# Seven block products in the second expert chunk, and the gate's first steps among the attention's last matmuls

## The chip, the core and the metric

One core of a Trainium2 chip runs one program. The time is what the device takes for it, in microseconds (us). TensorE (PE) multiplies matrices, VectorE (DVE), ScalarE (ACT) and GpSimd (POOL) work element by element, and SyncE (SP) issues most of the transfers from memory.

## The reference

Three layers in a row, all in float32: attention with sinks and a sliding window, a mixture of 8 experts whose weights P are normalised over rows and columns eight times, and a second two-layer network.

```python
scores = where(is_sink | in_window, q @ k.T / sqrt(D), -1e9)
a = exp(scores - max); a /= sum(a); x = a @ v            # 2 x 8 heads, 768 tokens, D = 64

P = exp(x @ w_gate - max)                                # 1536 tokens, 512 wide, 8 experts
for _ in range(8):
    P /= P.sum(1) + 1e-9; P /= P.sum(0) + 1e-9; P *= N / E
for e in range(8):                                       # w1: 512 x 1024, w2: 1024 x 512
    out += P[:, e] * (maximum(x @ w1[e], 0) @ w2[e])

g = maximum(out @ w_in, 0) ** 2                          # 512 x 2048
return g @ w_out
```

## The kernel before, in words

**Chunks and blocks.** The hidden width is cut into chunks of 512: 16 expert chunks (two for each expert) and 4 of the last network. The 1536 tokens are three blocks of 512 (t = 0, 1, 2). A chunk's first layer makes h from x and w1, the second layer adds h @ w2 to acc. Each float32 operand is kept as a high and a low part (`xh`, `xl`, weights `h`, `l`), and a product is three matmuls, high by high and the two mixed ones; `pair_split` (L467) makes such a pair with an ACT copy for the high part and a POOL subtraction for the low part.

**Plain and fast first layers.** `plain(c, t, f)` is one group of 12 matmuls of 512 columns: a quarter f of the chunk's width for block t. `fast(c, half, 0)` (L780) makes blocks 0 and 1 together for two quarters by seven block products (p1 to p7, 6 matmuls each) instead of eight, in the manner of Strassen and Winograd. It needs sums of weights (S1 to S4: `unit_sums` on POOL, then `units(c, half, 3, k)` splits them into pairs) and sums of x (T1 to T4: `sums(0)`, subtractions on DVE followed by a `pair_split`). Its additions are steps e1 to e7: e1 copies p1's bank to the scratch tile x0 on ACT, and p2 goes on adding in that bank; the others are DVE additions, and p3 and p4 go on adding in the banks that e5 and e7 read. Scratch tiles have one buffer for each tag ("x0", "x1", "x2", "u"); a tag's next tile waits until the last reader of the one before is done. `sums(1)` and `fast(c, half, 1)` do the same inside block 2.

**What is fast.** Chunk 0 runs among the attention's steps (phase_a, `filler`), in groups of 384 tokens. Chunk 1 is plain in all three blocks, in the order 1, 0, second layer of 1, then 2, second layer of 0 and 2. From chunk 2 on (`is_fast`) the first layer goes by products. The sums T of x are made during chunk 1, since all later expert chunks use the same x.

**Order of work.** It is written out by hand: every engine runs its instructions in the order in which the program issues them. In phase_b `run` goes through a list `seq` of PE groups; `plan[k]`, filled with `put(k, step)`, holds what is issued after group k. `gate()` (L933) is a generator of 13 pauses: three steps with 8 matmuls each for the logits, one for the largest logit, two more, and then the eight normalisations, one for each pause. `GATE_AT` lists after which groups its next step is issued. Its matmuls take the weights `wgz` (tag x0), made from the load `wgr` (tag x2) by an ACT copy and a DVE subtraction (L1304, L1305).

**The start of phase_b.** The loads' memory is that of the attention, so they start when its last matmuls have read theirs. `next_loads` issues the loads in the order of `load_list`, each into one of three buffers; load number k waits until number k - 3 has been used. Then `wgr` is issued. The `fill` loop issues what is left of chunk 0's matmuls; after each finished group it calls `evac` and one of four `units` steps. After it come the copies for `wgz`, then `run` with one plain group and the last three groups of chunk 0 (`rest`), then the list of chunk 1:

```python
        for _ in fill:                       # L1295
            if self.done:
                self.evac()
                if todo:
                    todo.pop(0)()
        ...
        gate = self.gate()                   # L1308
```

Of the kernel before, what the change touches and what calls it, by code (L numbers as in the profile page):

```python
# [10 lines left out]
F32 = mybir.dt.float32  # L11
# [3 lines left out]
AF = mybir.ActivationFunctionType  # L15
ALU = mybir.AluOpType
# [21 lines left out]
NC = NC1 + NC2  # L38
CONV = 3
CONV_AT = (0, 1, 2, 3, 8, 9, 10, 11, 12, 13, 14, 15)  # L40
GATE_AT = (0, 1, 2, 3, 5, 7, 9, 11, 13, 16, 19, 22, 25, 30)
W2_AT = (2, 5, 8, 11)
NB = 512
BIG = 1e30
# [4 lines left out]
class Kernel:  # L49
# [373 lines left out]
    def load_list(self, c0):  # L423

        loads, k = [(c0, which, half) for which in range(2) for half in range(2)], 0
        for c in range(c0, NC):
            wide = [(j, 2, 0) for j in range(k, min(k + CONV, 8 * NC2)) if c >= 2]
            k += len(wide)
            n = c + 1
            loads += wide[0:1]  # L430
            if n < NC:
                if self.is_fast(n):
                    loads += [(n, 3, 0), (n, 3, 1)]
                loads += wide[1:2] + [(n, 0, 0)] + wide[2:3] + [(n, 0, 1), (n, 1, 0), (n, 1, 1)]
            else:
                assert len(wide) < 2
        return loads
# [217 lines left out]
        o = 2 * NB * q + w * t  # L655
        return tuple(x[:, k : k + 2, o : o + w] for x in (self.xh, self.xl))

    def sums(self, q):

        nc = self.nc  # L660
        T = [
            self.tp.tile([128, 3, 2, NB >> q], F32R, tag=f"T{q}{t}", name=f"T{q}{t}")
            for t in "hl"
        ]
        self.T[q] = T

        def tt(o, a, b, op):
            if isinstance(o, str):
                o = self.scratch2(o)[:, 0 : NB >> q]
            nc.vector.tensor_tensor(out=o, in0=a, in1=b, op=op)  # L670
            return o

        B = {n: self.operand(n, q) for n in ("B11", "B12", "B21", "B22")}
        f32 = lambda n, hl, kc: B[n][hl].bitcast(F32)[:, kc]

        def put(name, kc, x):
            hi, lo = self.operand(name, q)
            self.pair_split(hi[:, kc], lo[:, kc], x)

        for kc in range(2):  # L680
            x = tt("x0", f32("B22", 0, kc), f32("B12", 0, kc), ALU.subtract)
            y = tt("u", f32("B22", 1, kc), f32("B12", 1, kc), ALU.subtract)
            yield
            t3 = tt("x2", x, y, ALU.add)
            put("T3", kc, t3)
            yield
        for kc in range(2):
            x = tt("x0", f32("B12", 0, kc), f32("B11", 0, kc), ALU.subtract)
            y = tt("u", f32("B12", 1, kc), f32("B11", 1, kc), ALU.subtract)
            yield  # L690
            t1 = tt(x, x, y, ALU.add)
            put("T1", kc, t1)
            yield
            t2 = tt("u", f32("B22", 0, kc), t1, ALU.subtract)
            tt(t2, t2, f32("B22", 1, kc), ALU.add)
            put("T2", kc, t2)
            yield
            t4 = tt("x2", f32("B21", 0, kc), t2, ALU.subtract)
            tt(t4, t4, f32("B21", 1, kc), ALU.add)
            put("T4", kc, t4)  # L700
            yield
# [564 lines left out]
    def phase_b(self, c0, first, fill):  # L1266
# [25 lines left out]
        nc.gpsimd.memset(self.ones, 1.0)  # L1292
        nc.sync.dma_start(out=wgr, in_=self.wg)
        todo = [partial(self.units, c0, half, 0, k) for half in range(2) for k in range(2)]
        for _ in fill:  # L1295
            if self.done:
                self.evac()
                if todo:
                    todo.pop(0)()
        self.evac()  # L1300
        for step in todo:
            step()
        hz = self.wgz[:, :, 0:E]
        nc.scalar.activation(out=hz, in_=wgr, func=AF.Copy)  # L1304
        nc.vector.tensor_tensor(  # L1305
            out=self.wgz[:, :, E : 2 * E], in0=wgr, in1=hz.bitcast(F32), op=ALU.subtract
        )
        gate = self.gate()  # L1308
        groups = itertools.count()

        def run(seq, plan):

            for k, g in enumerate(seq):
                g()
                for step in plan.get(k, ()):
                    step()
                if next(groups) in GATE_AT:
                    next(gate, None)

        conv = itertools.chain.from_iterable(self.wide(k) for k in range(8 * NC2))  # L1320
# [3 lines left out]
        for c in range(c0, NC):  # L1324
# [6 lines left out]

            off = 0
            if not low:
                run([self.plain(c, 1, 0), *rest], {})
                low = first.close() or True
                self.w2p = self.pool(left, "w2" + n)
                self.tp = self.pool(left, "T" + n)
                self.cp, self.T = self.pool(left, "c" + n), {}
                seq = [self.plain(c, t, f) for t in (1, 0) for f in range(KD)][1:]
            elif self.is_fast(c):  # L1340
                seq = self.fast(c, 0, 0) + self.fast(c, 1, 0)
            else:
                seq = [self.plain(c, t, f) for t in (1, 0) for f in range(KD)]
            for k in range(4):
                put(W2_AT[k] if self.is_fast(c) else k, self.part_w2, c, k)
            if c == NC1:
                x = [self.x2(2, kc) for kc in range(KD)]
                seq = sum(([s, *x[k : k + 1]] for k, s in enumerate(seq)), [])
            m = len(seq)
            if self.is_fast(c):  # L1350
                (a, b, *e), (f, g, *i) = (self.fast(c, half, 1) for half in range(2))
                if c < FAST2:
                    seq += self.second(c, 1) + [a, b, f, g]
                else:
                    seq += [a] + self.second(c, 1) + [b, f, g]
                early = 4 if c < FAST2 else 2
                for k, step in (
                    (early, e[0]), (early, e[5]), (early, e[4]), (4, e[6]), (5, e[1]), (5, e[2]),
                    (6, i[0]), (6, i[5]), (6, i[4]), (6, i[6]), (6, e[3]),
                    (7, i[1]), (7, i[2]), (7, i[3]),  # L1360
                ):
                    put(m + k, step)
            else:
                seq = seq + self.second(c, 1) + [self.plain(c, 2, f) for f in range(KD)]
            if c == NC1 - 1:
                x = [self.x2(t, kc) for t in (1, 0) for kc in range(KD)]
                seq += sum(
                    ([s, x[k]] for k, s in enumerate(self.second(c, 0) + self.second(c, 2))), []
                )
                wide = lambda k: m + k if k < 8 else m + 2 * k - 8  # L1370
            else:
                seq += self.second(c, 0) + self.second(c, 2)
                wide = lambda k: m + k
            if c in (FAST - 1, FAST2 - 1):
                t = self.sums(0)
                for k in range(13):
                    put(k if c < FAST else min(2 * k, k + 5), next, t, None)
                t = self.sums(1)
                for k in range(13):
                    put(m + 8 + k // 2, next, t, None)  # L1380
            if c + 1 < NC:
                if self.is_fast(c + 1):
                    for half in range(2):
# [105 lines left out]
```

## Time and profile before

| | us |
|---|---|
| runs before: median of 3 | 1380.14 (1380.13 to 1380.63) |
| profiled execution | 1378.92 |
| its span | 1377.1 |
| PE busy | 1363.8 (99%), 7105 matmuls |
| DVE busy | 953.6 (69%) |
| ACT busy | 453.8 (33%) |
| POOL busy | 501.8 (36%) |

The span is what the profiler saw between the first and the last instruction of that execution. Busy time is the union of an engine's instructions; waiting instructions are not counted. Matmuls overlap in PE's pipeline, so a matmul of 512 columns has a duration of about 0.39 us while the next one starts 0.23 us after it. In a row of a time line, "x4" is that many instructions in a row, and the bracket at the end tells how long the engine stood idle before them and which instruction ended that.

### The profile page before, as it was taken

The page shows a single profiled execution, that of the slowest core. Times are in us where ns is not written, and L with a number is a line of the kernel's source. Part 1 is how long each engine was busy: PE and PEld are TensorE (multiplying, and loading weights), DVE is VectorE, ACT ScalarE, POOL GpSimd, SP SyncE. Part 2 cuts the span into 40 slices and gives each one's busy share as a digit, 9 for nine tenths or more (in the row PEclk, how much of TensorE's full clock was granted, in tenths as well). Part 3 has the DMA queues.
Part 4 walks back from the last instruction along what each step waited for, and adds up shares of the span by engine and source line. Part 5 has one row for each costly group of instructions (what it writes and reads, how often), then busy time and mean ns, then how long its engine had stood idle before and what let it go on. Part 6 is the DMA issues. An engine that isn't in the chain of part 4 may idle for free.

```text
span 1377.1 us, 18909 instructions
## 1 busy us (share of the span) xinstructions
PE 1363.8 (99%) x7105; PEld 1142.8 (83%) x7105; DVE 953.6 (69%) x1884; ACT 453.8 (33%) x1007; POOL 501.8 (36%) x442
## 2 busy tenths in 40 slices
PE   8999999999999999999999999999999999999998
PEld 5777888888888888888888888888888888888887
DVE  8777368887777777777777768765454568866564
ACT  6776322322232222222232222222232243433331
POOL 4322136534343434424343434423343035543310
PEclk9999999999999999999999999999999999999999
DMA  5232210132313232232313232230102010111101
GB/s 205 82 87 73 78 31 31 62 103 65 124 54 112 77 95 85 92 107 68 117 54 121 71 96 81 92 107 32 61 32 77 16 62 16 62 52 57 46 24 72
DMA packets 61146, 102.53 MB, mean 74 GB/s; under 512 B 3956, under 2 KB 43252, under 8 KB 60788
## 3 DMA queue, kind: packets, MB, share of 16 engines
q1 hardware_dynamic: 61040, 101.22, 23.3%
q8 instruction: 58, 0.95, 0.3%
q14 instruction: 44, 0.36, 0.1%
q10 hardware_dynamic: 4, 0.00, 0.0%
HBM read 89.67 MB, written 11.53 MB: 73 GB/s over the span
## 4 chain that ended last, share of the span: by engine, by line
PE 79%; DVE 1%; ACT 0%; issue 0%; DVEq 0%; ACTq 0%
PE mm L900 42%; PE mm L749 36%; PE mm L917 0%; ACT tx L720 0%; DVE acc L640 0%; DVE tx L721 0%; ACT hh L732 0%; DVE tx L809 0%; DVE hl L733 0%; DVE acc L636 0%; DVE mm L721 0%; DVE raw L565 0%; ACT tx L823 0%; DVE raw L552 0%; DVE tu L809 0%
## 5 line engine op out<-in xcount | busy, mean ns | idle before, releaser
L900 PE MATMUL mm<-w2h,hh 128*128 128x512 f32 (+1 forms) x916 | 356.9, 390 | 0.0
L900 PE MATMUL mm<-w2l,hh 128*128 128x512 f32 (+1 forms) x916 | 355.9, 389 | 0.0
L900 PE MATMUL mm<-w2h,hl 128*128 128x512 f32 (+1 forms) x916 | 355.7, 388 | 0.0
L469 POOL TENSOR_TENSOR w2l<-raw,w2h 128x512 fp32r<-128x512 f32 x76 | 118.4, 1557 | 366.0 <-ACT w2h L468 364.1
L640 DVE SCALAR_TENSOR_TENSOR acc<-mm,P,acc 128x512 f32<-128x512 f32 x168 | 125.7, 748 | 135.5 <-PE mm L900 134.2
L900 PEld LDWEIGHTS mm<-w2h,hl 128*128 128x128 f32 x916 | 172.0, 188 | 35.8
L900 PEld LDWEIGHTS mm<-w2h,hh 128*128 128x128 f32 x916 | 172.1, 188 | 34.5
L900 PEld LDWEIGHTS mm<-w2l,hh 128*128 128x128 f32 x916 | 172.1, 188 | 34.4
L512 POOL TENSOR_TENSOR raw<-raw 128x256 f32<-128x256 f32 x136 | 125.5, 926 | 8.8 <-DVE m L544 0.8
L469 POOL TENSOR_TENSOR s0l<-raw,s0h 128x512 fp32r<-128x512 f32 (+1 forms) x36 | 45.5, 1265 | 199.5 <-ACT s0h L468 199.5
L717 ACT ACTIVATE hh<-tx 128x512 fp32r<-128x512 f32 (+1 forms) x112 | 58.9, 525 | 130.0 <-DVE tx L809 129.5
L809 DVE TENSOR_TENSOR tx<-mm,tu 128x512 f32<-128x512 f32 (+1 forms) x136 | 75.6, 556 | 20.9 <-PE mm L749 16.7
L809 DVE TENSOR_TENSOR tx<-mm,tx 128x512 f32<-128x512 f32 (+1 forms) x68 | 37.9, 557 | 56.8 <-PE mm L749 55.5
L727 DVE SCALAR_TENSOR_TENSOR hl<-tx,hh 128x512 fp32r<-128x512 f32 (+1 forms) x112 | 70.1, 626 | 9.8 <-ACT hh L717 9.8
L823 ACT ACTIVATE tx<-mm 128x512 f32<-128x512 f32 x34 | 20.4, 599 | 156.6 <-PE mm L749 154.7
L633 DVE TENSOR_TENSOR acc<-mm,acc 128x512 f32<-128x512 f32 (+1 forms) x49 | 33.2, 677 | 50.8 <-PE mm L900 50.5
L717 ACT ACTIVATE hh<-mm 128x512 fp32r<-128x512 f32 (+1 forms) x68 | 34.1, 502 | 99.7 <-PE mm L749 99.7
L823 ACT ACTIVATE txs<-mm 128x256 f32<-128x256 f32 x34 | 13.0, 382 | 151.3 <-PE mm L749 151.3
L469 POOL TENSOR_TENSOR a0l<-raw,a0h 128x512 fp32r<-128x512 f32 (+1 forms) x38 | 42.6, 1137 | 51.8 <-ACT a0h L468 47.5
L749 PE MATMUL mm<-xl,a1h 128*128 128x512 f32 (+1 forms) x172 | 60.3, 350 | 0.2 <-ACT tx L823 0.2
L749 PE MATMUL mm<-xl,a0h 128*128 128x512 f32 (+1 forms) x172 | 59.8, 348 | 0.0
L749 PE MATMUL mm<-xh,a0h 128*128 128x512 f32 (+1 forms) x172 | 59.8, 347 | 0.0
(262 smaller groups left out, 3149.8 us busy)
## 6 DMA issues: line engine op xcount, KB each, us to landing
raw<-w SPq DMA_DIRECT2D x110, 512.0 KB, 3.7
raw<-win SPq DMA_DIRECT2D x16, 512.0 KB, 4.0
w<-m SPq DMA_DIRECT2D x32, 256.0 KB, 4.6
raw<-wout SPq DMA_DIRECT2D x16, 512.0 KB, 4.1
raw<-qkv SPq DMA_DIRECT2D x8, 624.0 KB, 5.4
raw<-qkv SPq DMA_DIRECT2D x7, 464.0 KB, 4.0
out<-acc SPq DMA_DIRECT2D x11, 256.0 KB, 2.0
wraw<-w SPq DMA_DIRECT2D x2, 1024.0 KB, 5.5
```

The costliest lines, as they stand in the source:

```text
L469: self.nc.gpsimd.tensor_tensor(out=lo, in0=src, in1=hi.bitcast(F32), op=ALU.subtract)
L512: self.nc.gpsimd.tensor_tensor(out=o, in0=x, in1=y, op=op)
L633: nc.vector.tensor_tensor(out=a, in0=ps, in1=a, op=ALU.add)
L640: nc.vector.scalar_tensor_tensor(out=a, in0=ps, scalar=self.P[:, ti, e : e + 1], in1=a, op0=ALU.mult, op1=ALU.add)
L717: nc.scalar.activation(out=hh, in_=src, func=AF.Relu)
L727: nc.vector.scalar_tensor_tensor(out=hl, in0=src, scalar=0.0, in1=hh.bitcast(F32), op0=ALU.max, op1=ALU.subtract,)
L749: self.nc.tensor.matmul(out=ps, lhsT=w[:, kc], rhs=x[:, kc], start=start and k == 0, stop=(k == n - 1), skip_group_check=True,)
L809: nc.vector.tensor_tensor(out=v[name], in0=v[a], in1=v[b], op=ALU.add)
L823: nc.scalar.activation(out=v["s"], in_=v["a"], func=AF.Copy)
L900: self.nc.tensor.matmul(out=ps[:, d], lhsT=x[:, f, s], rhs=w[:, f, d], start=(n == 0), stop=(n == 11),)
```

## The change

Chunk 1's first layer now takes block 2 plain first (`run` starts with `plain(1, 2, 0)`), then its second layer, and then blocks 0 and 1 by the seven products. For that:

- `load_list` puts a second copy of w1's first half, `(1, 3, 0)`, third and one of its second half, `(1, 3, 1)`, sixth. They are summed in place by `unit_sums(1, half, k)` and split by `units(1, half, 3, k)`: half 0's sums before `run`, its splits at list positions 0 and 1, half 1's sums at 1 and 2 and its splits at 4 and 5. w2's four pieces are split at 0, 0, 1 and 1.
- `sums(0)` has a second order (`t1_first`): T1 for both halves of kc before `run`, then T2, T4, T3 for kc 0 and for kc 1, one at each of the positions 0 to 5. T3 is now made from T2, in tag x0.
- The copies for `wgz` and the gate's start stand ahead of the `fill` loop. The loop issues one gate step after each finished group, up to four; the other ten are at `GATE_AT[1]`. The count there takes in the first four groups, so 12 is list position 8 (p6 of half 0).
- `sums(1)` stays with the last eight groups of the chunk, and the unit steps for chunk 2 keep their distance to its end.

```diff
-GATE_AT = (0, 1, 2, 3, 5, 7, 9, 11, 13, 16, 19, 22, 25, 30)
+GATE_AT = (
+    (0, 1, 2, 3, 5, 7, 9, 11, 13, 16, 19, 22, 25, 30),
+    (12, 14, 16, 18, 20, 22, 25, 28, 31, 36),
+)
...
         loads, k = [(c0, which, half) for which in range(2) for half in range(2)], 0
+        if c0:
+            loads[2:2] = [(c0, 3, 0)]
+            loads.append((c0, 3, 1))
...
+        if t1_first:
+            for kc in range(2):
+                x = tt("x0", f32("B12", 0, kc), f32("B11", 0, kc), ALU.subtract)
+                tt(x, x, f32("B12", 1, kc), ALU.add)
+                tt(x, x, f32("B11", 1, kc), ALU.subtract)
+                put("T1", kc, x)
+            yield
+            self.T_tiles(q)
+            for kc in range(2):
+                t2 = tt("u", f32("B22", 0, kc), f32("B12", 0, kc), ALU.subtract)
+                tt(t2, t2, f32("B22", 1, kc), ALU.add)
+                tt(t2, t2, f32("B12", 1, kc), ALU.subtract)
+                put("T2", kc, t2)
+                yield
+                t4 = tt("x2", f32("B21", 0, kc), t2, ALU.subtract)
+                tt(t4, t4, f32("B21", 1, kc), ALU.add)
+                put("T4", kc, t4)
+                yield
+                t3 = tt("x0", t2, f32("B11", 0, kc), ALU.subtract)
+                tt(t3, t3, f32("B11", 1, kc), ALU.subtract)
+                put("T3", kc, t3)
+                yield
+            return
...
+        hz = self.wgz[:, :, 0:E]
+        nc.scalar.activation(out=hz, in_=wgr, func=AF.Copy)
+        nc.vector.tensor_tensor(
+            out=self.wgz[:, :, E : 2 * E], in0=wgr, in1=hz.bitcast(F32), op=ALU.subtract
+        )
+        gate, early = self.gate(), 0
         for _ in fill:
             if self.done:
                 self.evac()
                 if todo:
                     todo.pop(0)()
+                if early < 4:
+                    next(gate)
+                    early += 1
...
+        if c0:
+            for k in range(4 - early):
+                next(gate)
+            t0 = self.sums(0, True)
+            next(t0)
+            for k in range(2):
+                self.unit_sums(c0, 0, k)
...
-                run([self.plain(c, 1, 0), *rest], {})
+                run([self.plain(c, 1 + c0, 0), *rest], {})
...
-                seq = [self.plain(c, t, f) for t in (1, 0) for f in range(KD)][1:]
+                seq = [self.plain(c, t, f) for t in ((2,) if c0 else (1, 0)) for f in range(KD)]
+                seq = seq[1:]
...
+            mixed = c == c0 == 1
             for k in range(4):
-                put(W2_AT[k] if self.is_fast(c) else k, self.part_w2, c, k)
+                put((0, 0, 1, 1)[k] if mixed else W2_AT[k] if self.is_fast(c) else k,
+                    self.part_w2, c, k)
...
+            if mixed:
+                m += 18
+                put(2, self.finish)
+                seq += self.second(c, 2) + self.fast(c, 0, 0) + self.fast(c, 1, 0)
+                seq += self.second(c, 1)
+                for half in range(2):
+                    for k in range(2):
+                        if half:
+                            put(1 + k, self.unit_sums, c, half, k)
+                        put((k, 4 + k)[half], self.units, c, half, 3, k)
...
+            elif mixed:
+                seq += self.second(c, 0)
+                wide = lambda k: m - 8 + k
...
-                t = self.sums(0)
-                for k in range(13):
-                    put(k if c < FAST else min(2 * k, k + 5), next, t, None)
+                t = t0 if mixed else self.sums(0)
+                for k in range(7 if mixed else 13):
+                    put(min(2 * k, k + 5) if c == FAST2 - 1 else k, next, t, None)
...
-                    put(m + 8 + k // 2, next, t, None)
+                    put(m + (k // 2 if mixed else 8 + k // 2), next, t, None)
```

## Rows read from the trace of the kernel before

**Rows 1.** The page, part 1: engine, busy us, share of the span, instructions.

```profile
PE 1363.8 (99%) x7105; PEld 1142.8 (83%) x7105; DVE 953.6 (69%) x1884; ACT 453.8 (33%) x1007; POOL 501.8 (36%) x442
```

**Rows 2.** Waits of PE, 150 to 1377 us: us in total, times, longest.

```profile
PE mm L749 <- DVE tx L809: 0.6, 1, 0.6
PE mm L749 <- ACT tx L823: 0.2, 1, 0.2
```

**Rows 3.** The chain that ended last: start us, us, engine, line, matmuls.

```profile
309.97 19.04 PE mm L749 x84
```

**Rows 4.** Time line of PE: start us, us, line, out<-in, shapes (three moments).

```profile
152.26 0.40 PE L616 MATMUL mm<-w1h,hl 128*128 128x512 f32 x1
...
166.34 0.39 PE L940 MATMUL mm<-xl,wgz 128*128 128x512 f32 x1
...
184.50 0.39 PE L749 MATMUL mm<-xl,a1h 128*128 128x512 f32 x1
```

**Rows 5.** Time line of SyncE's queue, 148 to 160 us.

```profile
150.92 1.95 SPq L459 DMA_DIRECT2D raw<-w  x3
152.91 0.43 SPq L1293 DMA_DIRECT2D wgr<-wg  x1
```

**Rows 6.** Quarter-microsecond windows: busy us of each engine, granted clock, DMA share, GB/s.

```profile
157.75:158.00 0.25, 0.25 (x3) 0.25 (x2) 0.00 (x0) 0.25 (x2) 0.25 (x2) 1.00 0.16 44
158.00:158.25 0.25, 0.25 (x4) 0.25 (x3) 0.19 (x1) 0.25 (x2) 0.25 (x1) 1.00 0.00 0
```

**Rows 7.** Time line of ACT at the loads and at w2's first piece.

```profile
155.16 0.94 ACT L468 ACTIVATE a0h<-raw 128x512 fp32r<-128x512 f32 x2 [3.78 <-DMA raw<-w]
...
164.16 0.22 ACT L1304 ACTIVATE wgz<-wgr 128x32 fp32r<-128x32 f32 x1
...
185.19 0.62 ACT L468 ACTIVATE w2h<-raw 128x512 fp32r<-128x512 f32 x1
```

**Rows 8.** Time line of DVE: wgz, one addition, one gate step from start to end.

```profile
164.77 0.18 DVE L1305 TENSOR_TENSOR wgz<-wgr,wgz 128x32 fp32r<-128x32 f32 x1
...
185.94 1.79 DVE L670 TENSOR_TENSOR tx<-tx,tu 128x512 f32<-128x512 f32 x1
...
241.51 0.25 DVE L989 TENSOR_REDUCE cs<-mm 128x8 f32<-128x104 f32 x1
...
243.63 0.68 DVE L633 TENSOR_TENSOR acc<-mm,acc 128x512 f32<-128x512 f32 x1
```

**Rows 9.** Time line of POOL in chunk 1.

```profile
185.89 1.29 POOL L469 TENSOR_TENSOR w2l<-raw,w2h 128x512 fp32r<-128x512 f32 x1 [23.89 <-ACT w2h L468]
...
189.86 1.75 POOL L469 TENSOR_TENSOR T0l<-tx,T0h 128x512 fp32r<-128x512 f32 x1
```

**Rows 10.** Groups on POOL, 150 to 282 us: busy us, mean ns of one.

```profile
L512 POOL TENSOR_TENSOR raw<-raw 128x256 f32<-128x256 f32 x16 | 14.9, 932 | 0.9
```

**Rows 11.** Groups on DVE, 247 to 270 us (chunk 2's products), the same columns.

```profile
L727 DVE SCALAR_TENSOR_TENSOR hl<-tx,hh 128x512 fp32r<-128x512 f32 x4 | 3.1, 767 | 0.0
L809 DVE TENSOR_TENSOR tx<-mm,tu 128x512 f32<-128x512 f32 x4 | 2.8, 692 | 0.5 <-PE mm L749 0.3
L727 DVE SCALAR_TENSOR_TENSOR hl<-tu,hh 128x512 fp32r<-128x512 f32 x2 | 2.7, 1340 | 0.1
...
L727 DVE SCALAR_TENSOR_TENSOR hl<-mm,hh 128x512 fp32r<-128x512 f32 x2 | 1.4, 681 | 0.0
```

**Rows 12.** DMA issues, 150 to 158 us: count, KB each, median us to landing.

```profile
raw<-w SPq DMA_DIRECT2D x3, 512.0 KB, 4.7
```

**Rows 13.** Groups on ACT, 247 to 282 us.

```profile
L823 ACT ACTIVATE tx<-mm 128x512 f32<-128x512 f32 x2 | 1.2, 588 | 0.0
```

**Rows 14.** Time line of PE at the program's start.

```profile
4.11 0.58 PE L126 MATMUL mm<-nw_f,acc 1*128 1x2 f32 x2 [4.11 <-DVE nw_f L121]
...
9.57 1.11 PE L326 MATMUL ptp<-ident,p 128*128 128x128 f32 x4
...
16.27 0.66 PE L326 MATMUL ptp<-ident,p 128*128 128x128 f32 x4
```

More of the change, by code (lines that the diff above doesn't have):

```diff
@@ L656, in operand, with T_tiles @@
         return tuple(x[:, k : k + 2, o : o + w] for x in (self.xh, self.xl))
-    def sums(self, q):
-        nc = self.nc
-        T = [
+    def T_tiles(self, q):
+        self.T[q] = [
             self.tp.tile([128, 3, 2, NB >> q], F32R, tag=f"T{q}{t}", name=f"T{q}{t}")
@@ L664, in sums @@
         ]
-        self.T[q] = T
+    def sums(self, q, t1_first=False):
+        nc = self.nc
         def tt(o, a, b, op):
@@ L678, in put @@
             self.pair_split(hi[:, kc], lo[:, kc], x)
+        if t1_first:
[21 more added lines that the diff above has]
+            return
+        self.T_tiles(q)
         for kc in range(2):
@@ L1302, in phase_b @@
             step()
[L1303 to L1308, printed above, removed]
+        if c0:
[5 more added lines that the diff above has]
+                self.unit_sums(c0, 0, k)
         groups = itertools.count()
@@ L1316, in run @@
                     step()
-                if next(groups) in GATE_AT:
+                if next(groups) in GATE_AT[c0]:
                     next(gate, None)
@@ L1349, in phase_b @@
             m = len(seq)
-            if self.is_fast(c):
+            if mixed:
[8 more added lines that the diff above has]
+                        put((k, 4 + k)[half], self.units, c, half, 3, k)
+            elif self.is_fast(c):
                 (a, b, *e), (f, g, *i) = (self.fast(c, half, 1) for half in range(2))
```

## The prediction, made before the changed kernel was run

> **What bounds the kernel now.** I read the page's shares first, then who TensorE (PE) waited for, then the chain of work, then each engine in order of time around chunk 1. The shares show PE busy for 1363.8 of 1377.1 us [rows 1]. The waits show what that means after 150 us: in all the rest of the span PE stood still for other engines for 0.8 us [rows 2]. So everything from the last attention steps on is one dense row of matmuls, and the chain gives its pace: 84 matmuls of 512 columns in 19.04 us, 0.2267 us each [rows 3]. Two things follow. A matmul that goes is worth 0.227 us. And a wait put into PE's row is lost in full, as there is next to no idle time later that could swallow it.
>
> The sum below is made against the profiled execution (1378.92 us, span 1377.1); the median of the runs shown, 1380.14, lies 1.2 us above, and I add that at the end.
>
> **Matmuls removed.** In chunk 1 the first layer of blocks 0 and 1 was 8 plain groups of 12 matmuls = 96; seven products of 6 for each of two weight halves are 84. 12 fewer: 12 x 0.2267 = **-2.7 us**, all on PE's row. The gate's matmuls are only moved, and the two sets of sums for block 0/1 are made once, as before, only earlier.
>
> **The gate moved into the attention's last steps.** What counts is where its first matmul now stands on PE. In phase_b the fill loop's first turn finds a finished group at once (the one whose last matmul starts at 152.26), so evac, one units step and then gate step 0 are issued there; its 8 matmuls stand right behind 152.26 + 0.23 = 152.5 instead of at 166.34 [rows 4]. They need wgz, which needs the load wgr, the ScalarE (ACT) copy and a VectorE (DVE) subtraction. SyncE issues wgr fourth, at 152.91, behind three loads of 512 KB [rows 5]; those can't start earlier, as their memory is the attention's. The DMA engines are still moving these four transfers in the last quarter before 158.0 and are empty after it [rows 6]. In the kernel before nobody noticed: the copy was only asked for at 164.16 [rows 7]. Now PE stands in front of it. From 158.0 on: landing to ACT's start some 0.6 us (the first big load took 4.24 us from issue to the copy that waited for it [rows 5, 7]; 152.91 + 4.24 is 157.15, plus its place behind the others), 0.22 the copy [rows 7], 0.18 the subtraction [rows 8], handovers and the weight load 0.4: 159.4. PE is idle from 152.5 to 159.4, **+6.9 us**. Bounds: the third load of the first three is now a piece of w1 in shorter rows, and if that lets wgr land at 157.1 the wait is 5.6; if wgr takes another 0.4, 7.3. The fill groups that could cover it stand behind on the same engine. ACT and GpSimd (POOL) also wait here for wgr (hz is now ahead of the units splits on ACT), but they only feed chunk 1, 15 us later.
>
> T1 follows when the fill is over: two rounds of 3 DVE subtractions (0.69 [rows 11]), an ACT copy and a POOL subtraction (1.29 [rows 9]), some 4 us each, beside the four groups (plain, three of chunk 0) = 10.9 us of PE. Hidden; I cost it at nothing, and the first half's unit_sums on POOL behind it are also done before they are needed; without that cover 8 us would be late. SyncE gets two more loads, 0.65 us each to issue [rows 5]; chunk 2's first ones stand behind (1, 3, 1) and are not wanted before second(1, 1). Nothing.
>
> **POOL's queue in chunk 1.** Call P the end of the first plain group of the ordered list (184.50 in the profile before [rows 4]). ACT reaches w2's first piece only after that group's relu, POOL starts its low part at P + 1.4 [rows 7, 9]. From there the new order stands on POOL: 4 pieces of w2, 2 unit pieces of half 0, three T pieces of each kc (6), 2 unit pieces of half 1: 14 subtractions of 128x512 at 1.29 [rows 9] = 18.1; unit_sums of half 1, 4 x 0.93 = 3.7 [rows 10]; and in the middle of it a stop. unit_sums(1, 1) needs the load (1, 3, 1), which may be issued only when POOL has finished the units of half 0 (the buffer is theirs), and stands on POOL ahead of T4, T3 and all of kc 1: 4.3 us of waiting (4.24 to the copy for the first of a batch; the median of three is 4.7 [rows 7, 12]). The last T3 is out at P + 1.4 + 18.1 + 3.7 + 4.3 = P + 27.5.
>
> PE, unhindered, would have done two plain groups (5.4), second(1, 2) (10.9) and p1, p6, p5 (4.1) at P + 20.4 and then come to p2. p2 adds into the bank that e1 must first copy out; e1 writes tag x0, a single buffer whose last holder is that T3, so it runs at P + 27.5 and takes 0.59 [rows 13], with the handover 28.4: **+8.0 us** at p2. (w2's last low piece, at P + 9.2 against the P + 7 of its use, and T2's second half for p6 are inside these 8, not beside them.) Bounds: without the x0 tie, p7 still needs the same T3 at P + 21.8 and the loss is 5.7; with all 14 at the 1.75 of one row [rows 9], 14.4.
>
> That row stands beside DVE work, and the DVE addition of two SBUF operands at 185.94, with POOL's subtraction of 185.89 running, took 1.79 [rows 8, 9]. The Trainium skill (SBUF — State Buffer, "Who interferes with whom") says why: a VectorE instruction with two SBUF inputs and a GpSimd one that reads SBUF share a port, and the later one is shut out. The two rows agree with it; by the rule in its full weight the sum would be 6 us higher. I keep 1.29, and 14.4 as the bound, since most of DVE's reads in that stretch (low parts and sums into acc) have one operand in PSUM.
>
> **DVE in the fast products.** Plain blocks cost DVE only their low parts; the seven products add ten additions of 0.69 and read three of four results from SBUF. And the gate's remaining steps now lie at every second group there (counts 12 to 22, that is behind p6, p2 and p3 of half 0 and p1, p5 and p7 of half 1), one Sinkhorn step being 243.63 - 241.51 = 2.1 [rows 8]. From e6 at P + 28.4 to the low part that second(1, 1) reads last (block 1, f = 2), DVE has 10 additions 6.9; low parts 2 x 0.68 + 4 x 0.77 + 1.34 = 5.8 [rows 11]; gate steps 0.4 + 2.0 + 4 x 2.1 = 10.9: 23.6, to P + 52.0, and the last matmul 0.2 behind. PE from p2 at P + 28.4 needs 11 products and one group, 17.7, to P + 46.1. The three waits that this shows as are e5 before p3 and e7 before p4 in half 1 and the low parts before second: **+6.1 us**. Bounds: 0 if DVE's lag fits between the banks, 9 if five of the low parts take the 1.34 of one of them instead of 0.77. Behind it no more: DVE's sums(1), adds and three gate steps leave it some 4 us behind PE when chunk 2 begins, and PE has p1, p6 and p5 (4.1 us) there before it asks DVE for anything.
>
> **Sum.** -2.7 + 6.9 + 8.0 + 6.1 = +18.3: 1378.9 + 18.3 + 1.2 = **1398 us**.
>
> **The rivals.**
> - *PE stays dense (the other side).* Place: the first gate matmul at 152.5. If wgz is ready when PE gets there and POOL's list fits into the 20 us before p2, only the 12 matmuls are left and the 0.8 us of waits may go too: 1380.1 - 2.7 = 1377.4. It decides at wgr's landing: up to 152.5 nothing is lost, up to 155.2 the saved matmuls still pay for it. For it: PE's waits name no DMA [rows 2]. Against: wgr is issued after 152.5 [rows 5].
> - *The gate's wait alone.* POOL and DVE keep up because PE's stop gives them time: -2.7 + 6.9, 1384.3. Against: T1 is hung behind the fill, and POOL's list hangs on P, so the earlier stop does not help it.
> - *The queues alone.* wgr lands early, the rest as above: -2.7 + 14.1, 1391.5. Against as in the first.
> - *PE's clock falls in the stops.* Four transposes took 1.11 us at 9.57 and 0.66 at 16.27; PE had done nothing before 4.11 [rows 14]. So after idle time the array ran near the lower of its two levels (1.2 against 2.4 GHz), and work there took 1/0.6 of its time. If the stop before 159.4 does that, the fill's 18 us behind it could lose 7 us at most; I take half, 1402, and the stop before p2 can do the like. For it: the length of the stops. Against: the profile before has none so long after the start, so no row decides. The Trainium skill (TensorE: Matmul & The Clock Gate, Part 1) has this rule: idle time throttles the array, and only sustained work releases it.
> - *It does not do what it says* (the products fall back to plain): PE's count of matmuls would not fall by 12. The code gives no sign of it, and I give it no share.
>
> **How the numbers follow.** Forecast 0.58 (own range 1393 to 1404), clock 0.20, gate alone 0.10, queues alone 0.08, PE dense 0.04. The range that leaves out PE dense, gate alone and the highest clock and port cases is 1386 to 1408. A difference of 0.2% (2.8 us) is about what can be told from none here: PE dense lies at that bound: 0.03 of it counts as faster, and 0.01 with 0.02 of short gate waits as within 0.2%; slower 0.94.
>
> **What would show it.** Right: a PE gap from 152.5 to about 159.4 released by DVE's wgz; hz on ACT at about 158.6; a POOL gap of about 4 us before unit_sums of half 1, released by a DMA; ACT's e1 copy released by POOL's T0l; PE waits on ACT tx L823 and DVE L809 in chunk 1; chunk 2's first product about 18 us later than before. Wrong: gate matmuls running before 157, or p2 starting without a gap behind p5. The matmul count must be 12 lower either way.

## The result and the profile after

The changed kernel takes **1394.72 us** (median of 4 runs, 1393.42 to 1396.13) where the kernel before took 1380.14 (1379.63 to 1380.63) beside it: ratio 1.0110, 95% interval 1.0097 to 1.0122. It is 14.6 us slower; the forecast was 18 slower (1398, range 1386 to 1408). The profiled execution took 1396.13, 17.2 us over that of before. 1.44 us of these lie ahead of the first changed instruction: the last matmul before the gate starts at 153.70 instead of 152.26, since the first matmuls of the program ran longer at the slow pace (four of them took 1.33 us at 13.05 where the same four took 0.76 at 12.92; the profile gives a granted clock of 1.00 there in both). That part belongs to neither kernel: in the runs below this matmul starts anywhere from 152.07 to 153.70. From that matmul to chunk 2's first product it is 264.08 - 153.70 = 110.38 us where it was 246.90 - 152.26 = 94.64. The change therefore costs **15.74 us** in that stretch, and nothing is lost behind it. Chunk 2's first product before, and in the changed kernel:

```profile
246.90 0.39 PE L749 MATMUL mm<-xl,a0h 128*128 128x512 f32 x1
```

```profile
264.08 0.39 PE L780 MATMUL mm<-xl,a0h 128*128 128x512 f32 x1
```

Page part 1 of the changed kernel (columns as in [rows 1]): 12 matmuls fewer, PE busy 98%. Below it, the row of the chain that answers to [rows 3].

```profile
PE 1367.7 (98%) x7093; PEld 1143.2 (82%) x7093; DVE 961.4 (69%) x1894; ACT 457.5 (33%) x1013; POOL 514.6 (37%) x454
```

```profile
327.14 19.04 PE mm L780 x84
```

Waits of PE, 150 to 1400 us (us in total, times, longest), against 0.8 us in [rows 2]. Line numbers are up to 31 higher than before. Only the last of these waits, 0.6, is in [rows 2] too.

```profile
PE mm L971 <- DVE wgz L1328: 7.3, 1, 7.3
PE mm L931 <- POOL w2l L475: 3.6, 1, 3.6
PE mm L780 <- ACT tx L854: 1.2, 1, 1.2
PE mm L1016 <- DVE P L1011: 1.1, 2, 0.8
PE mm L780 <- DVE tx L840: 0.6, 1, 0.6
```

The first stop on PE's time line: the bracket tells how long PE stood and for whom. Behind it the next matmuls start 0.43 us apart (161.98 and the rows after it), ten in all, until they are 0.23 apart again.

```profile
153.70 0.40 PE L622 MATMUL mm<-w1h,hl 128*128 128x512 f32 x1
161.39 0.80 PE L971 MATMUL mm<-xl,wgz 128*128 128x512 f32 x1 [7.29 <-DVE wgz L1328]
161.98 0.63 PE L971 MATMUL mm<-xh,wgz 128*128 128x512 f32 x1
162.41 0.63 PE L971 MATMUL mm<-xl,wgz 128*128 128x512 f32 x1
...
165.82 0.46 PE L622 MATMUL mm<-w1h,hl 128*128 128x512 f32 x1
166.12 0.40 PE L622 MATMUL mm<-w1h,hh 128*128 128x512 f32 x1
```

ACT's copy for wgz, released by the load; SyncE had issued that load at 154.34.

```profile
160.88 0.23 ACT L1327 ACTIVATE wgz<-wgr 128x32 fp32r<-128x32 f32 x1 [8.06 <-DMA wgr<-wg]
```

Windows of 5 us (columns as in [rows 6]; the clock is the third figure from the end). PE did nothing in the first, and was granted 0.50, the lower of its two levels, in the second.

```profile
155.00:160.00 5.00, 0.00 (x0) 0.00 (x0) 0.00 (x0) 0.00 (x0) 0.00 (x0) 0.91 0.77 248
160.00:165.00 5.00, 3.61 (x9) 2.84 (x10) 0.79 (x2) 0.79 (x2) 1.27 (x1) 0.50 0.02 5
165.00:170.00 5.00, 5.00 (x23) 3.83 (x22) 0.69 (x1) 1.20 (x3) 1.44 (x2) 0.91 0.22 66
```

POOL's list in chunk 1, which answers to [rows 9]. P, the end of the first plain group of the list, is 195.5 here. The list starts at P + 1.4; POOL runs from s0l into the sums of half 1 without a gap; most of the later subtractions take 1.74, not 1.29; the last T3 ends at 222.2. The first row is SyncE's: the sixth load of the list, (1, 3, 1), is issued at 199.97.

```profile
199.97 0.55 SPq L465 DMA_DIRECT2D raw<-w  x1
```

```profile
196.94 3.01 POOL L475 TENSOR_TENSOR w2l<-raw,w2h 128x512 fp32r<-128x512 f32 x2 [2.29 <-ACT w2h L474]
...
206.20 1.28 POOL L475 TENSOR_TENSOR s0l<-raw,s0h 128x512 fp32r<-128x512 f32 x1
207.44 1.54 POOL L518 TENSOR_TENSOR raw<-raw 128x256 f32<-128x256 f32 x2
...
212.46 1.74 POOL L475 TENSOR_TENSOR T0l<-tx,T0h 128x512 fp32r<-128x512 f32 x1
...
220.96 1.27 POOL L475 TENSOR_TENSOR T0l<-tx,T0h 128x512 fp32r<-128x512 f32 x1
```

The copy e1 right behind it on ACT. p2 starts at 222.92, P + 27.4.

```profile
222.27 0.60 ACT L854 ACTIVATE tx<-mm 128x512 f32<-128x512 f32 x1 [1.75 <-POOL T0l L475]
```

DVE: in the stretch where POOL was idle (228.6 to 242) a gate step from its first operation (229.07) to the addition behind it (230.64), 1.57 us, and a low part; then the same low part with POOL at work.

```profile
229.07 0.26 DVE L1020 TENSOR_REDUCE cs<-mm 128x8 f32<-128x104 f32 x1
...
230.47 0.26 DVE L1011 TENSOR_TENSOR P<-P,rs 128x96 f32<-128x96 f32 x1
230.64 0.68 DVE L840 TENSOR_TENSOR tu<-mm,tu 128x512 f32<-128x512 f32 x1
...
232.03 0.69 DVE L758 SCALAR_TENSOR_TENSOR hl<-tu,hh 128x512 fp32r<-128x512 f32 x1
...
244.06 1.75 DVE L758 SCALAR_TENSOR_TENSOR hl<-tu,hh 128x512 fp32r<-128x512 f32 x1
```

### The profile page after: what moved, and what is told of

Its sections match the earlier page's. It is cut to its first block, busy times and chain, and to the rows that moved or that the text cites. A ratio compares the mean times of both kernels' runs of the same rounds, so it can differ in the third digit from the quotient of the medians.

```text
span 1394.3 us, 18922 instructions
## 1 busy us (share of the span) xinstructions
PE 1367.7 (98%) x7093; PEld 1143.2 (82%) x7093; DVE 961.4 (69%) x1894; ACT 457.5 (33%) x1013; POOL 514.6 (37%) x454
## 4 chain that ended last, share of the span: by engine, by line
PE 78%; DVE 0%; issue 0%; DVEq 0%
PE mm L931 41%; PE mm L780 36%; PE mm L948 0%; DVE acc L646 0%; DVE acc L642 0%; DVE raw L571 0%; DVE tx L840 0%; DVE tu L840 0%; DVE raw L558 0%; DVE acc L639 0%; DVE raw L567 0%; DVE raw L563 0%; DVEq L646 0%; DVE m L575 0%; DVEq L840 0%
## 5 line engine op out<-in xcount | busy, mean ns | idle before, releaser
L518 POOL TENSOR_TENSOR raw<-raw 128x256 f32<-128x256 f32 x144 | 130.3, 909 | 10.1 <-DMA raw<-w 1.2
L475 POOL TENSOR_TENSOR s0l<-raw,s0h 128x512 fp32r<-128x512 f32 (+1 forms) x38 | 49.0, 1290 | 210.4 <-ACT s0h L474 210.4
L840 DVE TENSOR_TENSOR tx<-mm,tu 128x512 f32<-128x512 f32 (+1 forms) x140 | 78.4, 560 | 21.2 <-PE mm L780 16.9
L475 POOL TENSOR_TENSOR a1l<-raw,a1h 128x512 fp32r<-128x512 f32 (+1 forms) x38 | 40.1, 1073 | 60.9 <-ACT a1h L474 60.9
L758 DVE SCALAR_TENSOR_TENSOR hl<-tu,hh 128x512 fp32r<-128x512 f32 (+1 forms) x58 | 59.4, 1024 | 1.5
L748 ACT ACTIVATE hh<-mm 128x512 fp32r<-128x512 f32 (+1 forms) x62 | 30.6, 493 | 90.9 <-PE mm L780 90.8
L208 POOL TENSOR_TENSOR qkl<-raw,qkh 128x672 fp32r<-128x672 f32 (+3 forms) x24 | 33.4, 1414 | 68.5 <-ACT qkh L207 68.5
```

The source lines that it names most:

```text
L208: nc.gpsimd.tensor_tensor(out=cut(lo), in0=cut(raw), in1=cut(hi.bitcast(F32)), op=ALU.subtract)
L475: self.nc.gpsimd.tensor_tensor(out=lo, in0=src, in1=hi.bitcast(F32), op=ALU.subtract)
L518: self.nc.gpsimd.tensor_tensor(out=o, in0=x, in1=y, op=op)
L748: nc.scalar.activation(out=hh, in_=src, func=AF.Relu)
L758: nc.vector.scalar_tensor_tensor(out=hl, in0=src, scalar=0.0, in1=hh.bitcast(F32), op0=ALU.max, op1=ALU.subtract,)
L840: nc.vector.tensor_tensor(out=v[name], in0=v[a], in1=v[b], op=ALU.add)
```

## The experiments

All ratios are to the kernel before, run on the same chip beside each kernel. The changed kernel was not run again beside them, so a difference to its 1394.72 us carries the drift between the groups of runs, in which the kernel before lay at 1379.3 to 1380.1. Where it matters, I compare the traces instead, over the stretch from the last matmul ahead of the gate to chunk 2's first product: 110.38 us in the changed kernel.

**The gate's weights ready in time (e1).**

```diff
+        self.wgr = self.gp.tile([128, KD, E], F32, name="wgr")      # 128 bytes of its own
...
             if u == 7:
                 self.w_load(0, 1)
+                nc.sync.dma_start(out=self.wgr, in_=self.wg)
```

> The changed kernel, but the gate's small weights are loaded during the attention into a tile of their own, so that the ACT copy and the DVE subtraction for wgz can run as soon as wgz's memory is free. Account of the profile: PE's 7.3 us stop before the first gate matmul goes, and with it the low clock behind it (10 matmuls at 0.43 instead of 0.23, 2.1 us): 1394.7 - 9.4 = 1385.3; the stop before w2's low part stays at 3.6 us, since POOL's list hangs on PE's position. Rival A, the pace behind the stop has another cause: 1387.4. Rival B, POOL's and DVE's lists hang on the clock on the wall and not on PE: the later stops grow by what is saved, 1392 or more.

1407.82 us (1407.16 to 1408.33), ratio 1.0204 (1.0190 to 1.0218): slower, although no wait on wgz is left. PE's pace had fallen everywhere: 84 matmuls took 19.60 us in the chain instead of 19.04. The new tile had moved all later tiles by 128 bytes. As it stands the experiment says nothing on the stop; e7 and e1b take the two apart.

**The address alone (e7, e11, e12).** The changed kernel, in which only the size of an unread pad tile ahead of the big tiles differs: 128 bytes more, 256 less, 512 less.

```diff
-PAD = 176
+PAD = 208        # e7;   112 in e11, 48 in e12
```

> The changed kernel with its pad tile 128 bytes larger and nothing else: every later tile lies 128 bytes further on in SBUF, no instruction is added or moved. Theory 'e1 was slowed by its addresses': 84 matmuls of 512 columns take 19.5 us instead of 19.04 in the chain as in e1, and the kernel takes 1394.7 + 22 = 1417 (1410 to 1420; e1's 1407.8 was without the gate's stop of 9.4). Rival 'addresses do not matter, e1 lost it in another way': 1394.7 as the changed kernel.

> The changed kernel with its pad tile 256 bytes smaller and nothing else. e7 showed 22 us for a shift by 128 bytes. If what counts is the place within 256 bytes, the pace stays 19.04 us for 84 matmuls and the time 1394.7; if every other address than the one chosen is slower, the pace is 19.5 and the time 1415 or so.

> The same with 512 bytes less. If the place within 512 bytes counts, this one keeps 19.04 us for 84 matmuls and e11 does not; if the place within 256 bytes counts, both keep it; if neither does, it depends on something longer and only the chosen address has the pace.

e7: 1416.17 us (1415.68 to 1416.84), ratio 1.0266 (1.0250 to 1.0282). e11: 1394.78, e12: 1395.47 (one run each). The first 84-matmul rows of their chains (start us, us, what) are, for e7 and then for e11:

```profile
327.12 19.52 PE mm L780 x84
```

```profile
326.20 19.04 PE mm L780 x84
```

With no instruction changed, a shift by 128 bytes costs 21.5 us, about what e1 lost beyond its gain, and shifts by 256 and 512 cost nothing. The three fit a rule by the place within 256 bytes, but only one place off by 128 bytes was tried (e1 has the same one). Which tile it is that must lie there was not tried.

**The gate's weights ready, addresses kept (e1b).** e1 with `PAD = 144`.

> As e1 (wgr loaded early into 128 bytes of its own, so that wgz is ready when the gate's first matmul comes), but the pad behind it is 128 bytes smaller, so that all tiles after it keep the addresses they have in the changed kernel. Theory 'the first stop': PE's stop of 7.3 us ahead of the gate goes, and with it the 2.1 us that ten matmuls at half pace cost behind it; POOL's list hangs on the first plain group and keeps its loss: 1394.7 - 9.4 = 1385.3 (1384 to 1387). Rival 'the early load itself slowed e1': the time stays near e1's 1407.8 although the addresses are kept. Rival 'given back later': the stops on POOL's w2l and at p2 grow by what the gate's stop had hidden: 1390 or more.

1386.53 us (1384.88 to 1386.71), ratio 1.0048 (1.0035 to 1.0062). The first theory holds: 8.2 us less than the changed kernel by the medians, where 9.4 were expected, and 9.3 by the stretch in the traces (101.07 us). PE's waits: no L971, and the others, the 0.6 of L780 on DVE tx among them, hardly changed, so that nothing of the first stop was given back later.

```profile
PE mm L931 <- POOL w2l L475: 3.6, 1, 3.6
PE mm L780 <- ACT tx L854: 1.3, 1, 1.3
PE mm L1016 <- DVE P L1011: 1.1, 2, 0.8
```

**The slow matmuls behind the stop (e2).** 32 matmuls of 512 columns whose result nobody reads, ahead of the gate's first one, so that PE doesn't stand still.

```diff
+                if c0 and early == 0:
+                    ps = self.mmtile()
+                    for k in range(32):
+                        nc.tensor.matmul(
+                            out=ps, lhsT=self.xh[:, 0, 0:128], rhs=self.xh[:, 1, 0:512],
+                            start=(k == 0), stop=(k == 31),
+                        )
                 if early < 4:
```

> The changed kernel with 32 matmuls of 512 columns, whose result nobody reads, put into PE's row ahead of the first gate matmul: at 0.227 us they fill 7.26 us, the length of the stop. If the slow matmuls behind the stop come from the array's idle time, they run at 0.227 here and the kernel is 2.1 us faster than the changed one although it does more: 1392.6. If they have another cause (the gate's operands, the DMA traffic), it is the same or slower: 1394.7 or more.

1392.64 us (1392.41 to 1393.21), ratio 1.0095 (1.0080 to 1.0111): 2.1 less, with the same wait for the load filled by useless work. The window in which the changed kernel had 0.50 has 1.00 here:

```profile
160.00:165.00 5.00, 5.00 (x26) 3.90 (x24) 0.26 (x1) 1.21 (x3) 2.34 (x3) 1.00 0.01 3
```

The two ratios' intervals overlap, so the traces have to carry this: from the gate's first matmul to the first of its second step PE took 4.98 us (160.01 to 164.99) where the changed kernel took 7.25 (161.39 to 168.64). Behind that two differences cancel: p2's stop is 0.4 instead of 1.2, and the slow stretch behind w2l is 0.8 longer.

So the stop cost its 7.3 us and some 2.1 more at half pace. The stop of 3.6 us at w2l has the same tail in the changed kernel: ten starts from 206.63 to 210.51 took 3.9 us where 2.3 is the pace, 1.6 more, and the granted clock falls to 0.50 there.

```profile
208.00:209.00 1.00, 1.00 (x4) 0.72 (x4) 0.65 (x2) 0.00 (x0) 0.92 (x3) 0.50 0.98 337
```

**POOL's list, shortened on POOL or only reordered (e3, e4).** e3 gives the low parts of T2, T4 and T3 to DVE, one step later; e4 splits all of w2 at position 0.

```diff
-                put("T2", kc, t2)                  # e3, and so for T4 and T3
+                flush()                            # DVE: the low part noted one step before
+                put2("T2", kc, t2)                 # ACT copy now, low part noted for DVE
...
-                put((0, 0, 1, 1)[k] if mixed else  # e4
+                put(0 if mixed else
```

> The changed kernel, with the low parts of T2, T4 and T3 made on DVE (one step later) instead of on POOL. Theory that POOL's list sets the stops in chunk 1: six of its 14 subtractions leave it, the last one is done near P + 17, before p2 (P + 20.4). The stop before second (3.6) shrinks to 2 or less, the one at p2 (1.2) and the second low-clock stretch (1.6) go: 1394.7 - 4.5 = 1390. Rival: DVE takes over as the bound, as it now waits for six ACT copies between its subtractions: 1394 or more.

> The changed kernel, with all four pieces of w2 at list position 0, so ahead of the unit pieces and T2 on POOL; nothing leaves the list. Theory that the length of POOL's list sets the loss up to p2: the stop at w2's low part falls from 3.6 to under 1, and T2 for p6 or T3's tile for p2 is late instead, by about 4 us in sum; only the second low-clock stretch may go: 1393. Rival, the place of w2 is what costs: 3.6 and the 1.6 behind it go, 1389.5.

e3: 1395.40 us (1393.60 to 1396.93), e4: 1396.07 (1394.96 to 1397.61), ratios 1.0110 and 1.0117, both no faster than the changed kernel. PE's waits in e3 (its lines are 17 further on), and in e4:

```profile
PE mm L797 <- ACT tx L871: 3.1, 1, 3.1
PE mm L948 <- POOL w2l L475: 1.9, 1, 1.9
```

```profile
PE mm L780 <- ACT tx L854: 4.0, 1, 4.0
PE mm L780 <- POOL T0l L475: 1.7, 1, 1.7
...
PE mm L931 <- POOL w2l L475: 0.2, 1, 0.2
```

Each time the stop at w2l shrinks and the one at p2 grows. In e3 the copy e1 is released by DVE:

```profile
220.64 0.60 ACT L871 ACTIVATE tx<-mm 128x512 f32<-128x512 f32 x1 [1.76 <-DVE T0l L698]
```

Both lists, POOL's and DVE's, are too long for what PE has to do between P and p2: POOL's takes 25.3 us in the changed kernel against PE's 20.4, and in e3 DVE is busy for 19.8 of the 20 us from 200 to 220. Moving an item from one to the other, or ahead of another one, moves the stop but does not shorten it.

**DVE's price with POOL at work (e8).** Eleven POOL subtractions of 128x512 that nobody reads, among the products.

```diff
+            if mixed:
+                def idle():
+                    d = self.tp.tile([128, 3, 2, 256], F32R, tag="T1l", name="idle")
+                    for k in range(11):
+                        nc.gpsimd.tensor_tensor(
+                            out=d[:, 0].rearrange("p k n -> p (k n)"),
+                            in0=self.xl.bitcast(F32)[:, 2, 0:512],
+                            in1=self.xh.bitcast(F32)[:, 2, 0:512], op=ALU.subtract,
+                        )
+                put(17, idle)
             run(seq, plan)
```

> The changed kernel with 11 additional POOL subtractions of 128x512 whose results nobody reads, in the stretch where blocks 0 and 1 go by products (POOL stood idle there from 228.6 to 242). The prediction had put 6.1 us of loss on DVE in that stretch, and 1.1 came. Theory 'its prices were those of a stretch with POOL running': with POOL busy DVE's operations with two SBUF operands get the longer times again (P<-P,rs 0.26 to 0.8 or more, hl<-tx and hl<-tu 0.69 to 0.8 and up to 1.75) and PE waits for DVE there: 1394.7 + 4 = 1399 (1397 to 1401), with waits of PE on DVE tx (L840) or DVE hl. Rival 'the lag fits between the banks at any price': DVE's times grow, but PE's waits do not: 1394.7 to 1396.

1399.66 us (1398.52 to 1401.70), ratio 1.0147 (1.0131 to 1.0162): 4.9 more, and 5.3 by the stretch in the traces (115.63 us). POOL's added row, DVE's rows that answer to 230.47 and 232.03 above, PE's wait for P, and the window behind its longest part:

```profile
226.24 15.99 POOL L1455 TENSOR_TENSOR idle<-xl,xh 128x512 fp32r<-128x512 f32 x11
```

```profile
228.76 0.75 DVE L1011 TENSOR_TENSOR P<-P,rs 128x96 f32<-128x96 f32 x1
...
230.04 1.28 DVE L758 SCALAR_TENSOR_TENSOR hl<-tx,hh 128x512 fp32r<-128x512 f32 x1
231.24 1.77 DVE L758 SCALAR_TENSOR_TENSOR hl<-tu,hh 128x512 fp32r<-128x512 f32 x1
```

```profile
PE mm L1016 <- DVE P L1011: 4.7, 3, 2.8
```

```profile
230.00:240.00 10.00, 7.17 (x24) 5.54 (x23) 9.19 (x17) 1.83 (x3) 9.45 (x8) 0.74 0.00 0
```

Both engines slow down: POOL's 11 take 1.45 each. Much of the lag that the prediction had priced at 6.1 us comes when POOL works there: the waits for P go from 1.1 to 4.7 (among the products alone, without the one in second(1, 1), from 0.3 to 3.8). Behind the longest one, 2.8 at 235.64, the granted clock of the window 230 to 240 is 0.74, and twelve matmuls took 5.26 us instead of 2.72. Against this 6.1 in all the first stop and its tail were about 1 us shorter in this execution. PE stands at the gate's steps, not at the low parts: the expected mechanism, in another place than the expectation had it (waits on tx or hl). The Trainium skill (SBUF — State Buffer, "Who interferes with whom") says that a VectorE instruction with two SBUF inputs contends with a GpSimd one that reads SBUF. These rows agree, 0.26 against 0.75 and 0.69 against 1.77 for the same shapes, and the rows with one input in PSUM don't move (0.68). Not every such instruction is hit: at 226.09 in the changed kernel P<-P,rs took 0.26 too, with POOL at chunk 2's sums.

**The gate as cover for POOL's list (e9, e10, e13).** The gate's first four steps leave the attention and stand behind the other plain groups, so that their 24 matmuls lie between P and p2 (in e13 16 of them); T3 is made before T4, and the copies for wgz stand behind the `fill` loop again. For that wgz has a tile of 32 columns of its own, and the pad is smaller by as much. e10 and e13 also move the splits of half 1's sums.

```diff
-    (12, 14, 16, 18, 20, 22, 25, 28, 31, 36),
+    (4, 5, 6, 7, 12, 14, 16, 18, 20, 22, 25, 28, 31, 36),      # e9
+    (4, 5, 6, 7, 12, 14, 16, 18, 21, 23, 25, 28, 32, 36),      # e10
+    (3, 4, 5, 6, 12, 14, 17, 20, 25, 28, 31, 34, 38, 42),      # e13
...
-                if early < 4:
-                    next(gate)
-                    early += 1
...
-                        put((k, 4 + k)[half], self.units, c, half, 3, k)
+                        put((k, 4 + 2 * k)[half], self.units, c, half, 3, k)      # e10
+                        put((k, 3 + 2 * k)[half], self.units, c, half, 3, k)      # e13
...
-                    put(min(2 * k, k + 5) if c == FAST2 - 1 else k, next, t, None)
+                    put((0, 1, 4, 4, 5, 6, 6)[k] if mixed else min(2 * k, k + 5), next, t, None)    # e9
+                    put((0, 1, 4, 4, 5, 7, 7)[k] if mixed else min(2 * k, k + 5), next, t, None)    # e10
+                    put((0, 1, 3, 3, 4, 7, 7)[k] if mixed else min(2 * k, k + 5), next, t, None)    # e13
```

> The changed kernel with the gate's four first steps taken out of the attention's last matmuls and put behind groups 4 to 7 of the count, that is behind the other plain groups and the first of second(1, 2); for that the gate's weights have a tile of their own (32 columns instead of 128 with zeros; the pad is smaller by as much, so later addresses are kept), and T3 is made before T4. Theory 'the gate's 24 matmuls (5.4 us) are cover for POOL's list': the first stop (7.3, with 2.1 of slow matmuls) goes, PE needs P + 25.8 to p2 instead of P + 20.4, T3's second half is out two subtractions earlier at about P + 24, so the stops on w2l (3.6, with 1.6 of slow matmuls) and at p2 (1.2) go too; what stays is DVE's 1.1 and some handovers against 2.7 of saved matmuls: 1379.5 (1378 to 1382), level with the kernel before. Rival 'DVE is late instead': T's sums wait behind the gate's copies on DVE, and p2 or p7 waits 2 us or more with a fall of the clock: 1383 or more.

> As e9, with what its trace showed mended: the copy e1 stood on ACT behind the high part of T4's second half, so that T4 goes behind e1 (position 7), the second split of half 1's sums goes behind T3 (position 6), and three of the gate's later steps come one group later, where PE had waited for P (counts 21, 23 and 32 instead of 20, 22 and 31). Theory 'e9's rest was these waits': the stop of 2.6 us at p2 goes, with some 1.2 us of slow matmuls behind it, and the 1.0 us on P: 1382.9 - 4.8 = 1378.1 (1377 to 1380), the 2.7 us of the saved matmuls below the kernel before less about 1. Rival 'DVE has no room': e6 and e5 come late behind T4's sums, p3 waits for e5, and the time stays at 1381 or above.

> As e10, with its three remaining stops taken on: the gate's first four steps stand one group earlier (counts 3 to 6), so that T4 and T3 of the second half start on DVE one group (2.7 us) earlier (positions 3 and 4) while 16 of the gate's 24 matmuls still lie between the first plain group of the list and p2; and the eight normalisations are spread further (17, 20, 25, 28, 31, 34, 38, 42), so that only two of them fall among the products and none right behind another. Theory 'e10's rest was DVE's place in the order': the stop at p2 (1.0), on P (1.5) and on hl (0.5) go: 1381.3 - 3.0 = 1378.3 (1377 to 1380). Rival 'the saved matmuls are always paid back on DVE or POOL': p2 waits for POOL's T3 again, as there are 8 gate matmuls (1.8 us) less to cover it, or chunk 2's products wait behind the later gate steps: 1381 or more.

e9: 1382.85 us (1380.83 to 1383.40), ratio 1.0021 (1.0012 to 1.0030), above the theory's bounds (1378 to 1382). The stops at the gate and at w2l are gone, as expected. One at p2 is left, since e1 stood on ACT behind the high part of T4, which had waited 2.75 us for DVE's sum, the rival's case:

```profile
PE mm L780 <- ACT tx L854: 2.6, 1, 2.6
PE mm L1016 <- DVE P L1011: 1.0, 2, 0.7
```

e10: 1381.32 (1380.15 to 1382.13), ratio 1.0013 (1.0004 to 1.0022), 3 us above what was expected and at the rival's 1381: the stop at p2 shrank, and others grew.

```profile
PE mm L1016 <- DVE P L1011: 1.5, 2, 1.1
PE mm L780 <- ACT tx L854: 1.0, 1, 1.0
PE mm L780 <- DVE tx L840: 0.6, 1, 0.6
PE mm L931 <- DVE hl L758: 0.5, 1, 0.5
```

e13: 1379.75 (1378.77 to 1380.69) against 1379.26 for the kernel before, ratio 1.0004 (0.9995 to 1.0013): level with it, 1.5 above the expectation and within its bounds. Two stops on DVE are left, at gate steps that stand behind other work of DVE. The longer one lies among chunk 2's products (the row below), the second half of the rival; the other lies behind p2, at 207.75:

```profile
PE mm L1016 <- DVE P L1011: 1.8, 1, 1.8
PE mm L1001 <- DVE nm L998: 0.9, 1, 0.9
```

```profile
249.69 0.45 PE L1016 MATMUL mm<-P,ones 128*128 128x117 f32 x2 [1.78 <-DVE P L1011]
```

They add up to 2.7 us, what the 12 matmuls save; a third stop, 0.6 on DVE tx, the kernel before has as well. No version here beats the kernel before.

## Why the prediction was right

The direction, the two main losses and the place of the first came as predicted; the second was foreseen at p2 alone and came in two places. Three terms were off and partly cancel: measured, and with P as the mark, -2.7 + 7.3 + 2.1 + 7.0 + 1.1 = 14.8 of the 15.7. The remaining 0.9 is in handovers of a few tenths that I did not settle one by one. That the total came within 3 us is in part luck: DVE's term was 5.0 too high, and against it stand 2.1 for the clock, which the sum leaves out, and this 0.9.

- **Matmuls removed, -2.7.** Right: 7093 against 7105, at an unchanged 19.04 us for 84 matmuls.
- **The gate's wait, +6.9.** Right: 7.3, released by DVE's wgz. The load took 6.5 us from its issue to the copy, 0.9 more than forecast; copy, subtraction and handover took 0.5 together instead of 0.8. Counted as the prediction counts, from 0.23 us behind the last matmul's start, the wait is 7.5. e1b shows that the whole term hangs on this load.
- **The clock.** This was given as a rival with 0.20 and left out of the sum. It came beside the forecast, and smaller than the half of 7 us that I had put on it: 2.1 us behind the first stop, shown by e2, and 1.6 behind w2l (inside the 7.0 below), read from the rows alone. The 7 was low for its premise: 18 us of work at 0.6 of the pace lose 12. And the slow pace at the program's start, from which the rival was read [rows 14], stands in the profile at a granted clock of 1.00, so that those rows show a pace and not the clock. The Trainium skill (TensorE: Matmul & The Clock Gate, Part 1) has idle time throttling the array; the granted 0.50 behind the first stop agrees.
- **POOL's list, +8.0.** The end was right: list from P + 1.4, last T3 at P + 26.7 (P + 27.5 forecast), p2 at P + 27.4 against P + 20.4 unhindered, 7.0. Inside, two parts were wrong. The DMA stop of 4.3 us does not exist: the load (1, 3, 1) was issued at 199.97, when POOL had done w2's second piece, and POOL came to it 7.5 us later, at 207.44 (the rows above): the buffer it waited for was w2's, not that of half 0's sums. In its place the 14 subtractions took 21.5 instead of 18.1, up to 1.74 each beside DVE's sums: towards the bound that the prediction named for the contention and did not choose. That the two nearly cancel is luck. And PE stopped first at second's w2l (3.6, with 1.6 of slow matmuls) and for only 1.2 at p2; e4 shows that this is one loss in two places. That the length of the list against PE's work decides is shown by e9, where 24 matmuls put between them take the stop at w2l away.
- **DVE in the products, +6.1.** The mis-sized term: 1.1, and only 0.3 of it lies in the products (the wait for P at 234.34); 0.8 is a gate step in second(1, 1) at 261.02, where the prediction had put nothing. The step that failed is its prices, 2.1 for a gate step and 1.34 for hl<-tu [rows 8, 11], which come from stretches with POOL running. In chunk 1 POOL stood idle from 228.6 to 242, and the same work took 1.57 and 0.69. e8 gives POOL something to do, and 3.5 us of waits for P come among the products. Prices are not all of it: with the changed kernel's own durations the prediction's list for DVE adds up to 19.3 us instead of 23.6, by my estimate a lag of 1.8. Why only 0.3 of that reached PE no run shows; the prediction's bound of 0, the lag that fits between the banks, is the likely reason.
- **Behind it nothing.** Right: the span's 17.2 us are all there at chunk 2's first product (17.18).

## What to carry to other kernels

Where one engine is dense, an instruction moved forward on it is priced by its latest input: find the load's issue in the queue before counting what the move saves. A side engine's list is compared with the work that the dense engine has in front of the first use; if the list is the longer one, reordering only moves the stop, and moving independent work of the dense engine in between takes it away. Take an operation's price from a stretch in which the other engines do the same kind of work.

## What the runs showed that I had not expected

The pace of PE depends on where the tiles behind the pad lie: 19.04 us for 84 matmuls of 512 columns at the chosen addresses and at 256 and 512 bytes less, 19.52 with 128 bytes more, and the whole kernel goes from 1394.7 to 1416.2. An edit that adds a small tile must keep the addresses behind it, or its time says something about the addresses instead.
